# The order of the first two matmuls of a couple of units in the second product of a feed-forward phase

## Chip, cores and metric

One core of one Trainium2 chip runs the whole program. The time is device microseconds of one execution; the figure for a kernel is the median over its runs, and one more execution, taken with the profiler, gives the trace.

## What is computed

For 2048 tokens of width 640, in float32: a layer norm without scale, local dilated attention with 32 heads of 20 (each token looks at 8 tokens, two apart, itself the first), and beside it a feed-forward network whose output, through a SiLU, gates the attention's output.

```python
xn = _layernorm(x, axis=-1)
s = _A_ref(xn, A_wqkv, A_wo)          # qkv, windowed softmax attention, output projection
g = _silu(_B_ref(xn, B_w1, B_w2))     # silu(xn @ w1) @ w2, hidden width 1536
return x + s * g
```

## The kernel before, in words

The tokens are cut into 4 groups of 512 (two halves of the sequence, odd and even tokens apart, since the attention steps by two), and each group into T = 4 tiles of 128 tokens. For each group the program runs a phase of the q, k and v products with the attention (`qkv_phase`), the output projection of the group before (`wo_phase`), and the feed-forward phase (`ffn_phase`); the last group's projection (`wo_last`) ends the program.

Every matrix product is made of three TensorE products, to keep float32 accuracy: each operand is split into a high and a low part, and high times high, low times high and high times low are summed in PSUM. A matmul's stationary operand is a 128 x 128 tile, loaded by a weight load of its own; the moving operand has 512, 384 or 256 columns.

The unit of weights is a block of 128 rows of a weight matrix with its two halves (`wh`, `wl`), in a ring of RING = 7 SBUF slots. Loads of later units go out as slots come free (`w_load`, line 397; from the second use on a DMA from GpSimd's queue, line 410).

`ffn_phase` (line 880) takes the 12 blocks of the hidden width two at a time; two blocks are a couple of units here. For a couple:

- `up(f)` (line 885), twice: 15 matmuls of 512 columns each (lines 893 to 895) make the block's 512 hidden values for all tokens in a `rot` bank of PSUM. ScalarE then writes SiLU of it to `sh` (line 899, the high part) and to `sf` (line 900); VectorE makes the low part `sl` (line 901).
- `down((f, f + 1))` (line 904): for both blocks and each of the 4 token tiles, `big` (line 911) multiplies the tile of `sh` with `wh` and with `wl`; then for both blocks `small` (line 922) multiplies `sl` with `wh`.

The output of a token tile has 640 columns, more than a PSUM bank holds, so each product with a weight half is a pair of matmuls, made by `tm_mm` (line 770): a wide piece of CA = 384 columns into a bank of the tile's own (line 774), and a narrow piece of CB = 256 columns into half of a bank that two tiles share (line 777). The argument `cols` says which of the two goes first:

```python
def tm_mm(banks, t, st, w, first, last, cols=(0, 1)):
...
    for k in cols:
        (wide, narrow)[k]()
```

A couple so has 24 pairs (16 of `big`, 8 of `small`), 48 matmuls behind 30 matmuls of 512 columns. Before the change every pair of `down` takes the wide piece first, but for the last pair of a couple, which takes the narrow one first (`ends`, line 923).

The order of the work is set by a planner, `Weave` (line 63): each step is added with its engine, an assumed duration, the keys that it reads and writes, and a priority. TensorE's steps stay in the order in which they were added; the other engines' are chosen by a simulated clock. A `big` is one step for the planner, whatever the order inside it. The steps behind an entry into `down` are in these groups: `first` (line 890) of the couple's second block, then `big` with t = 0 of the first block.

Of the kernel before, what the change touches and what calls it, by code (L numbers as in the profile page):

```python
# [54 lines left out]
def tsl(t):  # L55
    return slice(t * P, (t + 1) * P)
# [157 lines left out]
def local_attention_silu_ffn(ctx: ExitStack, tc: tile.TileContext, x, wqkv, wo, w1, w2, out):  # L214
# [84 lines left out]
    def act(n, fn, reads, writes, prio, table=None):  # L299
        add("ACT", ac(n), fn, reads, writes, prio, table=table)  # L300

    def pe(dur, fn, reads, writes):
        add("PE", dur, fn, reads, writes)
        clock[0] += dur
# [128 lines left out]
    def w_next(*want):  # L433

        i = used[0]
        assert units[i] == want and i < loaded[0], (units[i], want)
        used[0] += 1
        s, n = i % RING, width(want)
        return WR[s][:, :n], WR[s][:, n:2 * n], ("wh", s), ("wl", s)

    def w_done(n=1):
        for _ in range(n):
            w_load()
# [321 lines left out]
    def tm_banks(narrow_first=False):  # L765
        b = [bank() for t in range(T // 2)] if narrow_first else None
        a = [bank() for t in range(T)]
        return a, b or [bank() for t in range(T // 2)]

    def tm_mm(banks, t, st, w, first, last, cols=(0, 1)):  # L770
        a, b = banks
        h = t % 2
        def wide():
            nc.tensor.matmul(a[t][0][:, :CA], st, w[:, :CA], start=first, stop=last)  # L774

        def narrow():
            nc.tensor.matmul(b[t // 2][0][:, h * CB:(h + 1) * CB], st, w[:, CA:], start=first and h == 0,  # L777
                             stop=last, skip_group_check=True)
        for k in cols:
            (wide, narrow)[k]()  # L780
# [99 lines left out]
    def ffn_phase(g, i, ix, io):  # L880
        nxt = g + 1 if g + 1 < NG else None
        ps = tm_banks()
# [21 lines left out]
        def down(fs):  # L904
            ws = {f: w_next("w2", f) for f in fs}
            ko = [[a[t][1], b[t // 2][1]] for t in range(T)]
            for f in fs:
                sh, ksh = SH[f % 2], ("sh", f % 2)
                wh, wl, kh, kl = ws[f]
                for t in range(T):  # L910
                    def big(t=t, f=f, sh=sh, wh=wh, wl=wl):
                        tm_mm(ps, t, sh[:, tsl(t)], wh, f == 0, False)
                        tm_mm(ps, t, sh[:, tsl(t)], wl, False, False)
                    near = f == FC - 1 and t == 0
                    pe(2 * TM, big, [ksh, kh, kl], ko[t] + ["near"] * near)
                    if near:
                        act(1, lambda: nc.scalar.activation(SD[:, 0, 0:1], epst, AF.Silu), ["near"], [("sd", 0)], 0, "silu")
            for f in fs:
                sl, ksl = SL[f % 2], ("sl", f % 2)
                wh, wl, kh, kl = ws[f]  # L920
                for t in range(T):
                    def small(t=t, f=f, sl=sl, wh=wh):
                        ends = f == fs[-1] and t == T - 1
                        tm_mm(ps, t, sl[:, tsl(t)], wh, False, f == FC - 1, (1, 0) if ends else (0, 1))
                    pe(TM, small, [ksl, kh], ko[t])
                w_done()
# [64 lines left out]
```

## Time and profile before

| | |
|---|---|
| median of 3 runs | 620.53 us (619.21 to 621.4) |
| the profiled execution: its own time | 621.1 us |
| its span, from the first to the last instruction | 619.3 us |
| TensorE busy | 612.6 us, 3357 matmuls |
| VectorE busy | 562.9 us |
| ScalarE busy | 308.3 us |
| GpSimd busy | 113.4 us |
| mean DMA rate | 262 GB/s |

In the profile PE is TensorE's matmuls, PEld its weight loads, DVE VectorE, ACT ScalarE, POOL GpSimd and SP the queue that issues most DMAs. L774 is line 774 of the kernel; the helper `tm_mm` records both pieces of a pair there (L774 the wide one, L777 the narrow one), whoever calls it, so groups are told apart by the tile that they read: `sh` and `sl` are the second product of the feed-forward phase, `thl` the output projection or the q, k and v products. A row of the timeline has start, duration, engine, line and operation. A matmul's duration in it (279 to 390 ns) overlaps the next one's; the distance from one start to the next is what it takes of TensorE.

### The profile page before, as it was taken

To read this page: it belongs to the slowest core of one execution; us is meant where nothing else is said; L and a number is where in the kernel's file an instruction comes from. 1 tells how busy PE (TensorE), PEld (TensorE's weight loads), DVE (VectorE), ACT (ScalarE), POOL (GpSimd) and SP (SyncE) were. 2 spreads that over 40 slices of the span, in tenths; PEclk is the share of its full clock that TensorE was granted. 3 is DMA by queue.
4 is the path that set the end of the run, shared out by engine and by line. 5 is a ranking of instruction groups with operands and counts; after the bars stand their busy time and mean duration, and the time that the engine had idled before them with its cause. 6 is when DMAs were issued, how large, how long until landed. Compare 5 with 4: busy or idle time off the path is not lost.

```text
span 619.3 us, 9090 instructions
## 1 busy us (share of the span) xinstructions
PE 612.6 (99%) x3357; PEld 553.6 (89%) x3357; DVE 562.9 (91%) x581; ACT 308.3 (50%) x651; POOL 113.4 (18%) x168
## 2 busy tenths in 40 slices
PE   8999999999999999999999999999999999999997
PEld 7889899999889999999888999999988999999997
DVE  6449999999989999999998999999979999899974
ACT  5424657936476313861844602593396416153650
POOL 4510000001110133111222232311111213311100
PEclk9999999999999999999999999999999999999999
DMA  8989999876999997865699999865579999966642
GB/s 254 316 238 333 357 358 395 351 237 196 286 335 353 330 357 264 260 190 153 173 262 238 326 340 331 261 192 163 150 205 281 247 317 306 302 197 194 208 131 106
DMA packets 65449, 162.45 MB, mean 262 GB/s; under 512 B 7053, under 2 KB 29165, under 8 KB 65405
## 3 DMA queue, kind: packets, MB, share of 16 engines
q0 software_dynamic: 20016, 82.58, 44.6%
q1 hardware_dynamic: 45389, 79.29, 40.6%
q8 instruction: 26, 0.43, 0.3%
q14 instruction: 18, 0.15, 0.1%
HBM read 109.55 MB, written 34.16 MB: 232 GB/s over the span
## 4 chain that ended last, share of the span: by engine, by line
PE 88%; DMA 6%; SPq 3%; DVE 2%; issue 1%; ACT 0%; DVEq 0%
PE acc L774 22%; PE acc L777 14%; PE rot L895 8%; PE rot L894 8%; PE rot L893 8%; PE acc L747 8%; PE acc L746 8%; PE acc L745 8%; DMA half_q<-w 2%; DMA half_w<-w 1%; DMA kv<-kv 1%; SPq L384 1%; PE acc L684 1%; SPq L385 1%; DMA gate<-in_A_wqkv_dram 1%; PE rot L777 1%
## 5 line engine op out<-in xcount | busy, mean ns | idle before, releaser
L745 PE MATMUL acc<-w,thl 128*128 128x512 f32 (+1 forms) x300 | 112.5, 375 | 0.0
L747 PE MATMUL acc<-w,thl 128*128 128x512 f32 (+1 forms) x300 | 112.4, 375 | 0.0
L746 PE MATMUL acc<-w,thl 128*128 128x512 f32 (+1 forms) x300 | 112.4, 375 | 0.0
L774 PE MATMUL acc<-w,sh 128*128 128x384 f32 x384 | 111.6, 334 | 0.0
L777 PE MATMUL acc<-w,sh 128*128 128x256 f32 x384 | 107.1, 279 | 0.0
L899 ACT ACTIVATE sh<-rot 128x512 fp32r<-128x512 f32 x48 | 28.7, 597 | 150.2 <-PE rot L895 150.1
L895 PE MATMUL rot<-thl,w 128*128 128x512 f32 x240 | 93.6, 390 | 0.0
L894 PE MATMUL rot<-thl,w 128*128 128x512 f32 x240 | 93.6, 390 | 0.0
L893 PE MATMUL rot<-thl,w 128*128 128x512 f32 x240 | 93.5, 389 | 0.0
L617 DVE TENSOR_TENSOR pr<-e,kv 128x2560 f32<-128x2560 f32 x32 | 90.3, 2822 | 0.7
L579 DVE TENSOR_TENSOR pr<-q,kv 128x2560 f32<-128x2560 f32 x32 | 90.1, 2817 | 0.5 <-DMA kv<-kv 0.3
L582 DVE TENSOR_REDUCE l<-pr 128x128 f32<-128x2560 f32 x32 | 90.0, 2813 | 0.5
L622 DVE TENSOR_TENSOR pr<-pr 128x1280 f32<-128x1280 f32 x64 | 75.5, 1180 | 1.5
L774 PEld LDWEIGHTS acc<-w,sh 128*128 128x128 f32 x384 | 72.1, 188 | 1.1
L777 PEld LDWEIGHTS acc<-w,sh 128*128 128x128 f32 x384 | 72.2, 188 | 0.9
L410 POOL DMA_DIRECT2D w<-half_w x72 | 38.5, 534 | 188.0 <-PE rot L895 59.8
L410 POOL DMA_DIRECT2D w<-half_q x52 | 27.6, 531 | 239.9 <-PE rot L895 114.7
L745 PEld LDWEIGHTS acc<-w,thl 128*128 128x128 f32 x300 | 56.3, 188 | 8.9 <-ACT q L536 0.2
L746 PEld LDWEIGHTS acc<-w,thl 128*128 128x128 f32 x300 | 56.3, 188 | 8.7
L747 PEld LDWEIGHTS acc<-w,thl 128*128 128x128 f32 x300 | 56.3, 188 | 8.5
L774 PE MATMUL acc<-w,thl 128*128 128x384 f32 x225 | 63.1, 333 | 0.0
L495 ACT ACTIVATE xin<-sf 32x256 f32<-32x256 f32 (+1 forms) x144 | 54.6, 379 | 9.7 <-DVE sf L522 8.1
(92 smaller groups left out, 1042.7 us busy)
## 6 DMA issues: line engine op xcount, KB each, us to landing
w<-half_w POOLq DMA_DIRECT2D x72, 640.0 KB, 6.1
w<-half_q POOLq DMA_DIRECT2D x39, 512.0 KB, 4.7
half_w<-w SPq DMA_DIRECT2D x24, 640.0 KB
w<-half_wo POOLq DMA_DIRECT2D x15, 640.0 KB, 5.7
kv<-kv SPq DMA_DIRECT2D x15, 560.0 KB
half_q<-w SPq DMA_DIRECT2D x15, 512.0 KB
kv<-kv SPq DMA_DIRECT2D x15, 420.0 KB
gate<-in_B_w_dram SPq DMA_DIRECT2D x16, 320.0 KB
```

The costliest lines, as they stand in the source:

```text
L579: dve(2560, lambda t=t: nc.vector.tensor_tensor(out=PR, in0=win(qq[:, t:t + 2, :], W, 0), in1=win(kv[:, 0, t:t + 2, :], W, CQ), op=OP.mult ...
L582: dve(2560, lambda t=t: nc.vector.tensor_reduce(out=l[:, t:t + 2].rearrange("p t w h -> p (t w h)"), in_=PR.rearrange("p t w (h d) -> p (t ...
L617: dve(2560, lambda t=t, v=v: nc.vector.tensor_tensor(out=PR.rearrange("p t w (h d) -> p t (w h) d", d=DH), in0=e[:, t:t + 2].rearrange("p ...
L622: dve(2 * k * CQ, lambda k=k: nc.vector.tensor_tensor(out=PR[:, :, 0:k, :], in0=PR[:, :, 0:k, :], in1=PR[:, :, k:2 * k, :], op=OP.add), [] ...
L745: nc.tensor.matmul(o, hi, wh, start=c == 0, stop=False)
L746: nc.tensor.matmul(o, lo, wh, start=False, stop=False)
L747: nc.tensor.matmul(o, hi, wl, start=False, stop=c == DC - 1)
L774: nc.tensor.matmul(a[t][0][:, :CA], st, w[:, :CA], start=first, stop=last)
L777: nc.tensor.matmul(b[t // 2][0][:, h * CB:(h + 1) * CB], st, w[:, CA:], start=first and h == 0, stop=last, skip_group_check=True)
L893: nc.tensor.matmul(h, wh[:, cs], TH[i][:, c, :], start=c == 0, stop=False)
L894: nc.tensor.matmul(h, wh[:, cs], TL[i][:, c, :], start=False, stop=False)
L895: nc.tensor.matmul(h, wl[:, cs], TH[i][:, c, :], start=False, stop=c == DC - 1)
```

## The change

In `big`, the product of the high part with `wh` gets an order of its own. Where it is the very first pair of a couple (first block of the couple, first token tile) and the couple isn't the group's first one (`f` is not 0), the narrow piece goes ahead of the wide one. The pair behind it, with `wl`, keeps its order.

```diff
                     def big(t=t, f=f, sh=sh, wh=wh, wl=wl):
-                        tm_mm(ps, t, sh[:, tsl(t)], wh, f == 0, False)
+                        begins = f == fs[0] and t == 0 and f
+                        tm_mm(ps, t, sh[:, tsl(t)], wh, f == 0, False, (1, 0) if begins else (0, 1))
                         tm_mm(ps, t, sh[:, tsl(t)], wl, False, False)
```

Each group has 6 couples, of which 5 are changed: 20 in the program. VectorE's, ScalarE's, GpSimd's and SP's instructions stand as before.

TensorE, the second couple of group 0, before: the last two matmuls of `up`, then the couple's first pairs. `acc4` is the first token tile's own bank, `acc2` the one that it shares with the second tile, `w5` the ring slot of the couple's first unit, `sh0` the high part of its first block; in brackets the engines whose semaphores are waited for.

```order
L894 MATMUL rot1_112<-thl0_67,w4_78 128x512
L895 MATMUL rot1_112<-thl0_67,w4_78 128x512
L774 MATMUL acc4_109<-w5_79,sh0_82 128x384 [waits Activation_49]
L777 MATMUL acc2_107<-w5_79,sh0_82 128x256
L774 MATMUL acc4_109<-w5_79,sh0_82 128x384 [waits DVE_49]
L777 MATMUL acc2_107<-w5_79,sh0_82 128x256
L774 MATMUL acc5_110<-w5_79,sh0_82 128x384
```

TensorE at the same place, now:

```order
L894 MATMUL rot1_112<-thl0_67,w4_78 128x512
L895 MATMUL rot1_112<-thl0_67,w4_78 128x512
L777 MATMUL acc2_107<-w5_79,sh0_82 128x256 [waits Activation_49]
L774 MATMUL acc4_109<-w5_79,sh0_82 128x384
L774 MATMUL acc4_109<-w5_79,sh0_82 128x384 [waits DVE_49]
L777 MATMUL acc2_107<-w5_79,sh0_82 128x256
L774 MATMUL acc5_110<-w5_79,sh0_82 128x384
```

The first two of the couple have changed places, and the wait for ScalarE went to the one that is now first; the wait for VectorE (the low half of the weights) stays with the third. The wide bank is now written twice in a row.

TensorE, the second couple of group 1, before, where the weights come by a DMA (DMASW2 is its semaphore):

```order
L895 MATMUL rot_112<-thl_71,w_78 128x512
L774 MATMUL acc_107<-w_79,sh_82 128x384 [waits DMASW2_49,Activation_49]
L777 MATMUL acc_105<-w_79,sh_82 128x256
L774 MATMUL acc_107<-w_79,sh_82 128x384
L777 MATMUL acc_105<-w_79,sh_82 128x256
L774 MATMUL acc_108<-w_79,sh_82 128x384
```

TensorE at the same place, now:

```order
L895 MATMUL rot_112<-thl_71,w_78 128x512
L777 MATMUL acc_105<-w_79,sh_82 128x256 [waits DMASW2_49,Activation_49]
L774 MATMUL acc_107<-w_79,sh_82 128x384 x2
L777 MATMUL acc_105<-w_79,sh_82 128x256
L774 MATMUL acc_108<-w_79,sh_82 128x384
```

Both waits of the couple's first matmul went with its place, to the narrow piece. The 18 other changed entries have the same matmuls in the same orders; some lack the wait for VectorE or for the DMA.

## The prediction, made before the changed kernel ran

> **What bounds the kernel now.** I read the page first: the busy shares, the granted clock and the chain of work that ended last.
>
> ```profile
> span 619.3 us, 9090 instructions
> PE 612.6 (99%) x3357; PEld 553.6 (89%) x3357; DVE 562.9 (91%) x581; ACT 308.3 (50%) x651; POOL 113.4 (18%) x168
> PEclk9999999999999999999999999999999999999999
> PE 88%; DMA 6%; SPq 3%; DVE 2%; issue 1%; ACT 0%; DVEq 0%
> ```
>
> TensorE is busy in 99% of the span, at full granted clock in every slice, and 88% of the chain is TensorE work. VectorE's 91% looks close, but only 2% of the chain runs through it. The page warns that a busy PE is not a PE at its peak, because matmul ends are modelled; so every cost below is made from the start times of matmuls, not from their durations.
>
> Where does the rest of the chain lie? The chain in order of time shows its last DMA link, the last wait for VectorE, and the end:
>
> ```profile
> 64.79 9.13 DMA half_w<-w
> ...
> 74.05 0.69 DVE sl L901
> ...
> 611.36 2.60 PE acc L774 x15
> 613.95 1.72 PE acc L875 x15
> ```
>
> The last transfer in the chain ends at 64.79 + 9.13 = 73.92 us. From 74.8 to 615.7 us the chain is one unbroken row of matmuls. The first entry that the change touches is the second couple of group 0, in the timeline of TensorE:
>
> ```profile
> 83.81 0.39 PE L895 MATMUL rot<-thl,w 128*128 128x512 f32 x1
> 84.03 0.34 PE L774 MATMUL acc<-w,sh 128*128 128x384 f32 x1
> ```
>
> 84.03 us is behind that DMA. So each nanosecond that an entry gains or loses goes straight into the span: nothing hides it, and nothing else has to give way. The question is only how many nanoseconds the order of two matmuls is worth.
>
> The groups of instructions by line say whether TensorE ever waits at these lines:
>
> ```profile
> L774 PE MATMUL acc<-w,sh 128*128 128x384 f32 x384 | 111.6, 334 | 0.0
> L777 PE MATMUL acc<-w,sh 128*128 128x256 f32 x384 | 107.1, 279 | 0.0
> L774 PE MATMUL acc<-w,sl 128*128 128x384 f32 x192 | 57.4, 333 | 1.3 <-DVE sl L901 1.3
> ```
>
> The last column, idle time before the group, is 0.0 for all 768 matmuls that read `sh`, the first pair of every couple among them. The one wait of size (1.3 us) is in front of the `sl` matmuls, in the first couple of group 0, which the change leaves alone.
>
> **The change part by part.** In 5 of 6 couples of each of 4 groups, 20 in all, the first two matmuls change places. Nothing is added or removed: the same 48 matmuls, the same 48 weight loads, the same banks. TensorE's order goes from 512, 384, 256, 384, 256 to 512, 256, 384, 384, 256. No other engine's order moves, and no DMA.
>
> First, the wait that moves. It was on the 384-column piece and is now on the 256-column piece, which stands at the same place. What it waits for is ScalarE's `sh` of the couple's first unit, and past group 0 also the landing of that unit's weights. In the timeline of ScalarE:
>
> ```profile
> 217.89 0.60 ACT L899 ACTIVATE sh<-rot 128x512 fp32r<-128x512 f32 x1 [6.24 <-PE rot L895]
> ```
>
> That one ends at 218.49; the couple begins at 221.09 (below): 2.6 us to spare. For the landing there is no single row, but the 0.0 above covers it too. So the moved wait costs nothing before or after.
>
> Second, the spacing of the matmuls at an entry. This is the timeline of TensorE at the first couple of group 1 (its entry has the form of all 24); columns are start, duration, engine, line:
>
> ```profile
> 220.87 0.39 PE L895 MATMUL rot<-thl,w 128*128 128x512 f32 x1
> 221.09 0.34 PE L774 MATMUL acc<-w,sh 128*128 128x384 f32 x1
> 221.27 0.28 PE L777 MATMUL acc<-w,sh 128*128 128x256 f32 x1
> 221.39 0.34 PE L774 MATMUL acc<-w,sh 128*128 128x384 f32 x1
> 221.56 0.28 PE L777 MATMUL acc<-w,sh 128*128 128x256 f32 x1
> 221.68 0.34 PE L774 MATMUL acc<-w,sh 128*128 128x384 f32 x1
> ...
> 222.25 0.33 PE L774 MATMUL acc<-w,sh 128*128 128x384 f32 x1
> ```
>
> The fifth pair starts at 222.25, so the first four pairs took 222.25 - 221.09 = 1.16 us. To see what four pairs take undisturbed, I sum TensorE over stretches; the first is a stretch of 50 pairs in the output projection (the x in a column counts also the one or two matmuls that still run at its start), the second is a couple's 24 pairs, the third the 30 matmuls of 512 columns behind it, the fourth the next couple's 24 pairs:
>
> ```profile
> 199.76:214.09 14.33, 14.33 (x102) 14.33 (x101) 14.16 (x10) 7.48 (x16) 2.11 (x4) 1.00 1.10 337
> 221.09:227.99 6.90, 6.90 (x50) 6.89 (x49) 6.78 (x9) 1.09 (x2) 1.75 (x3) 1.00 1.07 406
> 227.99:234.81 6.82, 6.82 (x31) 5.63 (x31) 6.21 (x10) 1.09 (x2) 1.06 (x2) 1.00 0.95 303
> 234.81:241.71 6.90, 6.90 (x50) 6.89 (x49) 6.86 (x8) 3.95 (x5) 3.19 (x3) 1.00 0.71 250
> ```
>
> 14.33 / 50 = 0.2866 us for a pair; four make 1.146. The entry thus carries 1.160 - 1.146 = 0.014 us over the undisturbed stream. The whole down half of a couple carries 6.90 - 24 x 0.2866 = 0.02 us. That is all there is to win: at most 20 x 0.02 = 0.4 us, even if the new order made the half perfect. The 512-column half behind it begins 48 matmuls later, is preceded by the same matmuls as before, and doesn't change.
>
> What will the entry cost instead? Nowhere in this trace does a 256-column matmul follow a 512-column one, so I bound it by two rows. The nearest is the output projection, which enters with its narrow piece first, though out of a stream of 384:
>
> ```profile
> 197.06 0.28 PE L777 MATMUL acc<-w,thl 128*128 128x256 f32 x1
> ...
> 198.21 0.28 PE L777 MATMUL acc<-w,thl 128*128 128x256 f32 x1
> ```
>
> Four pairs take 198.21 - 197.06 = 1.15 us, 0.004 over the stream. If the new entry did as well, it would gain 0.010 us, times 20 = 0.2 us. The other end is an entry out of 512 columns into several 384-column matmuls on one bank, as the last quarter of the q, k and v products has it (here six of them), since the new order also puts two 384-column matmuls on one bank behind each other:
>
> ```profile
> 186.63 0.33 PE L745 MATMUL acc<-w,thl 128*128 128x384 f32 x1
> ...
> 187.70 0.33 PE L745 MATMUL acc<-w,thl 128*128 128x384 f32 x1
> ```
>
> Six steps take 1.07 us; undisturbed, by the chain's row above, six take 6 x 2.60 / 15 = 1.04. So this entry carries 0.03 us, 0.016 more than the present one; times 20 that is a loss of 0.3 us. Same-bank neighbours cost nothing by themselves: 2.60 / 15 = 0.1733 us there, against 0.17 to 0.18 for a 384-column step in the alternating rows.
>
> The sum runs from -0.4 to +0.3 us. I take -0.1: the narrow-first row is nearer in form (-0.2), but its step down in width is smaller than the one from 512, which speaks for less. Against the profiled execution's own time that is 621.1 - 0.1; the profiled execution lies 0.6 above the median of the runs shown, 620.53, and inside their spread, 619.21 to 621.4. So from the median: 620.5 - 0.1 = 620.4 us.
>
> Third, the weight load that stands behind a shorter matmul. The loads, from the page and from the timeline of PEld:
>
> ```profile
> L774 PEld LDWEIGHTS acc<-w,sh 128*128 128x128 f32 x384 | 72.1, 188 | 1.1
> 221.27 0.19 PEld L774 LDWEIGHTS acc<-w,sh 128*128 128x128 f32 x1
> 221.39 0.19 PEld L777 LDWEIGHTS acc<-w,sh 128*128 128x128 f32 x1
> ```
>
> Each load starts with the matmul in front of the one it serves. Now the couple's second load has the 384-column step, 221.27 - 221.09 = 0.18 us, to hide in; afterwards it has a 256-column step, 221.39 - 221.27 = 0.12. A load shows 0.188 us, more than either, yet the pairs keep to 0.2866 us, and the loads start 0.12 us apart and overlap one another in the records. So the 0.188 is latency, not occupancy, and a 256-column step hides a load already, in every pair. I cost this at nothing; if the cover failed, it is the second rival.
>
> The Trainium skill (TensorE: Matmul & The Clock Gate, section LDWEIGHTS) gives a load as the number of its columns divided by 1.2 GHz: an estimate of 107 ns for these 128 columns. By that the load fits under a 256-column step with some 10 ns left and the rival would cost nothing; a rule that speaks against putting a short matmul ahead of a load stops just short of biting here. By the recorded 188 ns the rival would cost 1.5 us.
>
> **The rivals.** One: no measurable change, which is the forecast; it takes in everything from -0.4 to +0.3 us, that is 620.1 to 620.8. What a measurement of this kernel can tell from no change is about 0.3%, 1.86 us, which is 1.86 / 20 = 0.093 us for each entry, six times what an entry carries now. Chance 0.93 (with it, that the change does less than it says: the first couples keep their order, so 20 of 24 entries move).
>
> Two, slower: the second load of the couple no longer hides. Behind a switch of tiles, from 512-column matmuls to a new `sh` and new weights, the load may not run as far ahead as in a steady stream. If its recorded 188 ns must fit under the 0.12 us step, 0.188 - 0.115 = 0.073 us come out for each entry, 20 x 0.073 = 1.5 us, 622.0, still under the bound. If it can't overlap at all, 20 x 0.188 = 3.8 us, 624.3. It decides from 0.093 us an entry on. For it: the one pair of widths that no row shows. Against it: in the entry of now the load at 221.27 sits under a 256-column matmul too, three matmuls behind the switch, and that step was 0.12 us like all others. Chance 0.03 for the full size.
>
> Three, faster by over 0.3%: it would need 0.093 us an entry, and the whole half holds 0.02. It can only come from elsewhere: the chain's DMA links, all before 74 us, differ from one execution to the next (the three runs span 2.2 us), without this change. Chance 0.03, and 0.01 more on the slow side for the same reason.
>
> **How the numbers follow.** Forecast 620.4 us. The range is set by the scatter of the runs more than by the change: from the lowest run, 619.2, to the highest with the upper bound of the cost added, 621.4 + 0.3 = 621.7. The second rival at full size lies outside with its 0.03. Faster by over 0.3%: 0.03; within: 0.93; slower: 0.04.
>
> **What would show it.** In the profile after, an entry should read 512, 256, 384, 384, with four pairs in 1.13 to 1.18 us, and a couple's 24 pairs in 6.88 to 6.92 us; idle before both `sh` groups stays 0.0, and the couple begins each 13.72 us (234.81 - 221.09) as now, to 0.02. The step behind the couple's first 256-column matmul tells of the second rival: about 0.12 us if the load hides, 0.19 and more if not. I am wrong if an entry moves by 0.093 us, or if idle time appears in front of a couple's first matmul.

## The result, and the profile after

The changed kernel takes 624.76 us (median of 4 runs, 624.61 to 625.38), the kernel before 620.2 us (median of 4, 619.21 to 621.4): a ratio of 1.0072, 95% interval 1.0052 to 1.0093. It is slower, by more than the 0.3% that a measurement of this kernel can tell. The forecast was 620.4 us and no change, at a chance of 0.93; the result lies outside the range.

The page of the changed kernel shows no new wait. TensorE has as many matmuls as before and is as busy (99%), at the same granted clock, in a span that is 3.8 us longer:

```profile
span 623.1 us, 9090 instructions
PE 617.5 (99%) x3357; PEld 558.8 (90%) x3357; DVE 561.7 (90%) x581; ACT 309.0 (50%) x651; POOL 112.9 (18%) x168
PEclk9999999999999999999999999999999999999999
PE 89%; DMA 6%; SPq 3%; DVE 1%; issue 1%; ACT 0%; ACTq 0%; DVEq 0%
```

The groups of the second product: idle time ahead of the `sh` matmuls is still 0.0, but the mean of one has grown, 334 to 340 ns for the wide piece, 279 to 281 for the narrow one. The third row stands for `sl`, whose matmuls the change doesn't touch; they went from 333 to 341.

```profile
L774 PE MATMUL acc<-w,sh 128*128 128x384 f32 x384 | 112.3, 340 | 0.0
L777 PE MATMUL acc<-w,sh 128*128 128x256 f32 x384 | 108.0, 281 | 0.0
L774 PE MATMUL acc<-w,sl 128*128 128x384 f32 x192 | 59.2, 341 | 0.1
```

Now an entry, in the timeline of TensorE (the third couple of group 1; columns start, duration, engine, line; the row with x2 is the two wide pieces in a row):

```profile
248.53 0.39 PE L895 MATMUL rot<-thl,w 128*128 128x512 f32 x1
248.76 0.28 PE L777 MATMUL acc<-w,sh 128*128 128x256 f32 x1
248.88 0.51 PE L774 MATMUL acc<-w,sh 128*128 128x384 f32 x2
249.22 0.28 PE L777 MATMUL acc<-w,sh 128*128 128x256 f32 x1
...
249.93 0.34 PE L774 MATMUL acc<-w,sh 128*128 128x384 f32 x1
```

The entry itself is as forecast: four pairs in 249.93 - 248.76 = 1.17 us (1.16 before), and the step from the first narrow piece to the wide one is 0.12 us, as in every other pair, so the weight load that runs beside it adds nothing. The time went elsewhere. This is the end of the same couple, 40 matmuls later:

```profile
254.42 0.34 PE L774 MATMUL acc<-w,sl 128*128 128x384 f32 x1
254.60 0.28 PE L777 MATMUL acc<-w,sl 128*128 128x256 f32 x1
254.72 0.34 PE L774 MATMUL acc<-w,sl 128*128 128x384 f32 x1
254.90 0.28 PE L777 MATMUL acc<-w,sl 128*128 128x256 f32 x1
255.02 0.34 PE L774 MATMUL acc<-w,sl 128*128 128x384 f32 x1
```

From wide piece to wide piece it is 0.30 us, 0.18 and 0.12, where it was 0.2866 before. The sums over the fifth to the last pair of this couple, in the kernel before and in the changed one (from left: the stretch, its length, busy PE, busy PEld):

```profile
249.69:255.43 5.74, 5.74 (x43) 5.74 (x42) 5.51 (x4) 5.66 (x9) 0.53 (x1) 1.00 0.73 236
```

```profile
249.93:255.93 6.00, 6.00 (x43) 6.00 (x42) 5.75 (x5) 5.91 (x10) 0.53 (x1) 1.00 0.66 210
```

5.74 / 20 = 0.287 us a pair before, 6.00 / 20 = 0.300 now. So there are two steady rhythms of the same alternating matmuls, at the same clock and without idle time, 13 ns a pair apart; the changed couples run in the slower one to their end. A whole couple's 24 pairs take 7.17 us in place of 6.89. The sum over the 24 pairs of a changed couple of group 1:

```profile
234.76:241.93 7.17, 7.17 (x50) 7.17 (x48) 7.10 (x9) 3.95 (x5) 2.91 (x3) 1.00 0.67 219
```

All 20 changed couples start in the slow rhythm, and 19 keep it: 19 x 0.274 = 5.2 us. Against that stands the first couple of group 0, which the change doesn't touch and whose start and wait differ from trace to trace: that couple's half took 8.47 us in the profiled execution before and 7.29 in the one after, 1.2 us less, and the couple began 0.24 us earlier (at 68.74 and 68.50 us). 5.2 - 1.2 - 0.2 = 3.8 us, the difference of the spans. Put otherwise, from the end of that couple on the program takes 542.1 us before and 547.3 after.

The twentieth changed couple is the most telling. It is the fourth of group 1, where TensorE stalls for a moment in both kernels, at the start of the couple's second block. Here are the matmuls of the changed kernel, and below them ScalarE's `sh` of that block and the weight load of the block's first piece:

```profile
264.51 0.34 PE L774 MATMUL acc<-w,sh 128*128 128x384 f32 x1
264.70 0.28 PE L777 MATMUL acc<-w,sh 128*128 128x256 f32 x1
264.81 0.34 PE L774 MATMUL acc<-w,sh 128*128 128x384 f32 x1
265.00 0.28 PE L777 MATMUL acc<-w,sh 128*128 128x256 f32 x1
265.11 0.43 PE L774 MATMUL acc<-w,sh 128*128 128x384 f32 x1
265.38 0.28 PE L777 MATMUL acc<-w,sh 128*128 128x256 f32 x1
...
265.78 0.33 PE L774 MATMUL acc<-w,sh 128*128 128x384 f32 x1
265.95 0.28 PE L777 MATMUL acc<-w,sh 128*128 128x256 f32 x1
266.06 0.33 PE L774 MATMUL acc<-w,sh 128*128 128x384 f32 x1
```

```profile
264.44 0.60 ACT L899 ACTIVATE sh<-rot 128x512 fp32r<-128x512 f32 x1
...
265.09 0.19 PEld L774 LDWEIGHTS acc<-w,sh 128*128 128x128 f32 x1
```

Up to 265.11 wide pieces begin 0.30 us apart; that one takes 0.27 to the next matmul, a stall of 0.08; from 265.78 on they begin 0.28 to 0.29 apart. The load had waited for `sh`, which was ready at 264.44 + 0.60 = 265.04 us: it begins 0.09 us behind the matmul at 265.00, where elsewhere a load is recorded 2 to 4 ns behind the matmul ahead of it. Behind this stall the fast rhythm was back.

### The profile page after: what moved, and what is told of

The parts are those of the page before. It is cut to its first block, busy times and chain, and to the rows that moved or that the text cites. A ratio compares the mean times of both kernels' runs of the same rounds, so it can differ in the third digit from the quotient of the medians.

```text
span 623.1 us, 9090 instructions
## 1 busy us (share of the span) xinstructions
PE 617.5 (99%) x3357; PEld 558.8 (90%) x3357; DVE 561.7 (90%) x581; ACT 309.0 (50%) x651; POOL 112.9 (18%) x168
## 4 chain that ended last, share of the span: by engine, by line
PE 89%; DMA 6%; SPq 3%; DVE 1%; issue 1%; ACT 0%; ACTq 0%; DVEq 0%
PE acc L774 22%; PE acc L777 14%; PE rot L895 8%; PE rot L894 8%; PE rot L893 8%; PE acc L745 8%; PE acc L746 8%; PE acc L747 8%; DMA half_q<-w 3%; DMA half_w<-w 1%; DMA kv<-kv 1%; SPq L384 1%; SPq L385 1%; PE acc L684 1%; PE rot L777 1%
## 5 line engine op out<-in xcount | busy, mean ns | idle before, releaser
L622 DVE TENSOR_TENSOR pr<-pr 128x1280 f32<-128x1280 f32 x64 | 73.9, 1155 | 1.5
L777 PEld LDWEIGHTS acc<-w,sh 128*128 128x128 f32 x384 | 72.2, 188 | 0.9
L774 PEld LDWEIGHTS acc<-w,sh 128*128 128x128 f32 x384 | 70.6, 187 | 1.0
L774 PE MATMUL acc<-w,sl 128*128 128x384 f32 x192 | 59.2, 341 | 0.1
```

Of the source, the lines that this page charges most:

```text
L622: dve(2 * k * CQ, lambda k=k: nc.vector.tensor_tensor(out=PR[:, :, 0:k, :], in0=PR[:, :, 0:k, :], in1=PR[:, :, k:2 * k, :], op=OP.add), [] ...
```

## The experiments

Each was one execution with a profile, beside one of the kernel before (619.06 to 620.17 us). Their whole times are told, but the first couple of group 0 moves them by up to 3.3 us: it began at 67.96 to 69.63 us and its half took 6.89 to 8.50, so that it ended at 74.85 to 78.13 us over all traces. So the verdicts rest on the lengths of couples and projections, and several totals lie outside the range of the very theory that the lengths bear out. W, N and B stand for matmuls of 384, 256 and 512 columns. "Changed couples" are the 20 past a group's first; the other 4 keep the order of before in every kernel, and ran at 6.89 us where nothing stalled and nothing was moved in memory.

### What of the new order does it: the two wide ones in a row, or the narrow one first?

**All pairs narrow first** (B, N W, N W, ...). In `big` and `small`, for couples past the first:

```diff
-                        tm_mm(ps, t, sh[:, tsl(t)], wh, f == 0, False)
-                        tm_mm(ps, t, sh[:, tsl(t)], wl, False, False)
+                        cols = (1, 0) if fs[0] else (0, 1)
+                        tm_mm(ps, t, sh[:, tsl(t)], wh, f == 0, False, cols)
+                        tm_mm(ps, t, sh[:, tsl(t)], wl, False, False, cols)
...
-                        tm_mm(ps, t, sl[:, tsl(t)], wh, False, f == FC - 1, (1, 0) if ends else (0, 1))
+                        tm_mm(ps, t, sl[:, tsl(t)], wh, False, f == FC - 1, (1, 0) if ends or fs[0] else (0, 1))
```

> All 24 pairs of the 20 changed couples take the narrow piece first, so a 256-column matmul still stands behind the last 512-column one, but no two wide pieces stand in a row. Theory A (two wide matmuls in a row move the stream into a slower rhythm, 0.300 us a pair in place of 0.287, that holds to the couple's end): the rhythm stays at 0.287, a couple's 24 pairs take 6.87 to 6.92 us, the whole 619 to 621.5. Theory B (the narrow matmul behind the 512-column one does it): 0.300 us a pair, 7.15 to 7.20 us for 24 pairs, the whole 624 to 626.

Measured: 624.3 us; the last 16 pairs of the second couple of group 1:

```profile
236.26:241.06 4.80, 4.80 (x34) 4.80 (x33) 4.73 (x8) 1.79 (x3) 1.00 (x2) 1.00 0.52 191
```

4.80 / 16 = 0.300. There are no two wide pieces in a row in these couples, so theory A falls; B stands.

**A turned pair in the middle** (B, W N, W N, W N, W N, N W, W N, ...):

```diff
-                        tm_mm(ps, t, sh[:, tsl(t)], wh, f == 0, False)
+                        turned = f == fs[0] and t == 2 and f
+                        tm_mm(ps, t, sh[:, tsl(t)], wh, f == 0, False, (1, 0) if turned else (0, 1))
```

> The couple begins wide first as before; the one turned pair is the high-weight pair of the third token tile, so that the stream has two narrow and then two wide pieces in a row at the fifth pair. Theory A in its plain form (any two wide in a row): 0.287 us a pair up to there and 0.300 from there on, 20 pairs by 0.0133 = 0.25 us for a couple more, the whole 624 to 626. Theory A in its balance form (a wide double moves the rhythm one way, a narrow double back): no lasting change, 6.88 to 6.93 us for 24 pairs. Theory B: 0.287 all along, 619 to 621.5.

Measured: 621.14 us, 24 pairs in 6.89 us; the last 16:

```profile
237.16:241.75 4.59, 4.59 (x35) 4.59 (x33) 4.55 (x7) 1.86 (x3) 1.10 (x2) 1.00 0.53 197
```

4.59 / 16 = 0.287. A turned pair inside a running stream does nothing, which again speaks against the plain form of A.

**The second wide piece on another bank** (the second token tile's pair with `wh` goes ahead of the first tile's pair with `wl`):

```diff
+                        if f == fs[0] and f and t < 2:
+                            tm_mm(ps, t, sh[:, tsl(t)], wh, f == 0, False, (0, 1) if t else (1, 0))
+                            if t:
+                                tm_mm(ps, 0, sh[:, tsl(0)], wl, False, False)
+                                tm_mm(ps, 1, sh[:, tsl(1)], wl, False, False)
+                            return
```

> The couple begins narrow, wide, wide, narrow as the changed kernel does, but the second wide piece belongs to the second token tile, so that the two wide ones write different PSUM banks and read the same moving operand. Theory A and theory B both: 0.300 us a pair as in the changed kernel, about 7.17 us for 24 pairs, 624 to 626. Theory C (the double write to one bank does it): 0.287, 6.88 to 6.92 us, 619 to 621.5.

Measured: 624.44 us, 24 pairs in 7.16. It doesn't matter whether the two wide pieces write one bank; C falls.

**Turned back at once** (B, N W, W N, N W, N W, ...): as the changed kernel, and all pairs behind the second one narrow first.

```diff
+                        begins = f == fs[0] and t == 0
+                        tm_mm(ps, t, sh[:, tsl(t)], wh, f == 0, False, (1, 0) if fs[0] else (0, 1))
+                        tm_mm(ps, t, sh[:, tsl(t)], wl, False, False, (1, 0) if fs[0] and not begins else (0, 1))
...
-                        tm_mm(ps, t, sl[:, tsl(t)], wh, False, f == FC - 1, (1, 0) if ends else (0, 1))
+                        tm_mm(ps, t, sl[:, tsl(t)], wh, False, f == FC - 1, (1, 0) if ends or fs[0] else (0, 1))
```

> The couple begins narrow, wide, wide, narrow as the changed kernel does, and all later pairs are narrow first, so that two narrow pieces in a row follow at once and the wide double is taken back. Theory A, plain form: 0.300 us a pair to the couple's end, about 7.17 us for 24 pairs, 624 to 626. Balance form: back at 0.287 after the narrow double, 6.88 to 6.93 us, 619 to 621.5. Theory B: 0.300, about 7.17 us.

Measured: 626.47 us, 24 pairs in 7.17. So within a couple, two wide pieces and then two narrow ones leave the slow rhythm as it is, and two narrow and then two wide ones (the second experiment) the fast one. The balance form falls too.

### What stands ahead

**The last 512-column matmul cut into two of 256**, with the changed order (B, N N, N W, W N, ...):

```diff
-                    nc.tensor.matmul(h, wl[:, cs], TH[i][:, c, :], start=False, stop=c == DC - 1)
+                    if f % 2 and f > 1 and c == DC - 1:
+                        for k in range(2):
+                            nc.tensor.matmul(h[:, k * 256:(k + 1) * 256], wl[:, cs],
+                                             TH[i][:, c, k * 256:(k + 1) * 256], start=False, stop=k == 1)
+                    else:
+                        nc.tensor.matmul(h, wl[:, cs], TH[i][:, c, :], start=False, stop=c == DC - 1)
```

> The changed kernel, with the last 512-column matmul ahead of the 20 changed couples cut into two of 256, so that the couple's narrow first piece stands behind a 256-column matmul; the arithmetic is the same. Theory B (a narrow piece directly behind a 512-column matmul sets the slow rhythm): 0.287 us a pair, 6.87 to 6.92 us for 24 pairs, the whole 619 to 622. Theory B2 (it is the narrow-first start of the couple, with its new tiles and waits, whatever stands ahead of it): 0.300 us a pair, 7.15 to 7.20 us, 624 to 626.

Measured: 624.31 us, 24 pairs in 7.16. It was to separate B from B2 and didn't quite: the first half of the cut is itself a 256-column matmul behind a 512. The runs on the cut below settle it.

**One 512-column matmul more, in mid-couple**, its result thrown away: ahead of the second block of the changed kernel, which then begins wide first, and ahead of the second block of the kernel before, which then begins narrow first (`begins = f == fs[1] and t == 0 and fs[0]`). The added step:

```diff
+                if f == fs[1] and fs[0]:
+                    pe(0.0, lambda sh=sh, wh=wh: nc.tensor.matmul(
+                        ROT[0], sh[:, tsl(0)], wh[:, :TOK], start=True, stop=True), [ksh, kh], [("rot", 0)])
```

> The changed kernel with one more 512-column matmul ahead of the couple's second block in the 20 changed couples; its result is thrown away, and the block then begins wide first. Theory B: the first 8 pairs run at up to 0.300 us, the 512 sets the rhythm anew, and the pairs behind it run at 0.287; the 16 of them take 4.59 to 4.62 us. Theory B2 (a slow rhythm lasts until the couple ends): 0.300 to the end, the 16 pairs take 4.78 to 4.81 us. The added matmuls cost 20 x 0.23 = 4.5 us by themselves, so the whole is 625 to 627 by B and 629 to 631 by B2.

Measured: 629.12 us; the 16 pairs behind the added matmul take 4.80 us: the slow rhythm stays, in all of these couples but the one that stalls.

> The kernel before (couples begin wide first), with the same added 512-column matmul ahead of the second block, whose very first pair is then narrow first. Theory B: 0.287 us a pair up to the added matmul, 0.300 behind it; the 16 pairs behind it take 4.74 to 4.81 us, the whole 627 to 630. Theory B2 (only the entry into the couple matters): 0.287 to the end, 4.58 to 4.62 us, 624 to 626.

Measured: 626.88 us. The entry into the second block, and the 16 pairs behind it:

```profile
236.86 0.28 PE L777 MATMUL acc<-w,sh 128*128 128x256 f32 x1
236.98 0.39 PE L911 MATMUL rot<-w,sh 128*128 128x512 f32 x1
237.21 0.28 PE L777 MATMUL acc<-w,sh 128*128 128x256 f32 x1
237.32 0.51 PE L774 MATMUL acc<-w,sh 128*128 128x384 f32 x2
```

```profile
237.21:241.97 4.76, 4.76 (x33) 4.76 (x32) 4.69 (x8) 1.64 (x3) 0.86 (x2) 1.00 0.48 175
```

4.76 against 4.59: with a 512 and a narrow piece behind it the fast rhythm became the slow one, in mid-couple. The added matmul is the first that reads the second block's `sh` and weights, and it takes over the wait for them, so the narrow piece has neither a wait nor new tiles of its own. So it is no matter of the couple's beginning as such (B2 falls here). No run begins the second block narrow first without the 512, so what the 512 adds is not shown. And a 512 and a wide piece did not turn the slow one back (B missed there): the two directions are not alike.

One of the 20 went another way, again the fourth couple of group 1, where the stall now falls on the added matmul. Its entry, and the 16 pairs behind it:

```profile
265.27 0.50 PE L911 MATMUL rot<-w,sh 128*128 128x512 f32 x1
265.61 0.28 PE L777 MATMUL acc<-w,sh 128*128 128x256 f32 x1
265.73 0.51 PE L774 MATMUL acc<-w,sh 128*128 128x384 f32 x2
```

```profile
265.61:270.20 4.59, 4.59 (x34) 4.59 (x32) 4.29 (x5) 4.50 (x8) 0.53 (x1) 1.00 0.27 103
```

The 512 took 0.34 us in place of 0.23, and with the same order of pieces behind it the pairs stayed at 4.59 / 16 = 0.287. So a narrow piece behind a 512 does not always bring the slow rhythm.

**The output projection wide first**, everything else as before:

```diff
-                    tm_mm(banks, t, OH[i][:, c, tsl(t)], wh, c == 0, False, (1, 0))
-                    tm_mm(banks, t, OH[i][:, c, tsl(t)], wl, False, False, (1, 0))
+                    tm_mm(banks, t, OH[i][:, c, tsl(t)], wh, c == 0, False)
+                    tm_mm(banks, t, OH[i][:, c, tsl(t)], wl, False, False)
...
-                    tm_mm(banks, t, OL[i][:, c, tsl(t)], wh, False, c == DC - 1, (1, 0))
+                    tm_mm(banks, t, OL[i][:, c, tsl(t)], wh, False, c == DC - 1)
```

> The feed-forward phase is as in the kernel before; the output projection of groups 0 to 2, which follows a stream of 384-column matmuls and took its narrow pieces first, takes its wide ones first in all of its 75 pairs. Theory B, as it stands (a narrow piece behind 512 columns): nothing changes, 0.287 us a pair, 619 to 621.5. Theory B3 (the piece that differs more in width from what stands ahead sets the fast rhythm in one case and the slow one in the other: it is wide first that is slow behind 384 columns): 0.300 us a pair in 3 x 75 pairs, 3 us more, 622 to 624.5.

Measured: 621.65 us. A projection has 60 pairs (5 blocks of 12), not the 75 of the expectation. Its 60 pairs of group 0, before (narrow first) and here of group 1 (wide first):

```profile
197.06:214.27 17.21, 17.21 (x122) 17.21 (x122) 17.01 (x11) 10.13 (x24) 2.63 (x5) 1.00 1.10 344
```

```profile
347.01:365.00 17.99, 17.99 (x121) 17.99 (x121) 16.19 (x17) 2.45 (x6) 2.65 (x5) 1.00 1.15 355
```

17.21 / 60 = 0.287 and 17.99 / 60 = 0.300: the same two rhythms, but here, behind 384-column matmuls, it is wide first that is slow. The other two projections of each kernel took the same. B as it stood explains nothing of this; the outcome is that of B3. But wide first behind a 384-column matmul isn't slow everywhere: the last projection, whose order no kernel changes, begins so behind the last couple's final wide piece, and it ran at 0.287 us a pair in both of these kernels.

### Where the tiles lie

The kernel places `sh`, `sl` and the projection's stationary tiles 64 bytes past a multiple of 128 in each partition (the projection's by SHIFT = 16 columns, `sh` by what is allocated ahead of it); the weights start on multiples of 128. Does that matter? First 64 bytes of padding ahead of `sh`, under the changed order and under the order of before:

```diff
+    pad = sb.tile([P, 16], F32, name="pad")
     SH = tiles("sh", 2, [P, TOK], F32R)
```

> The changed kernel with 64 bytes of padding ahead of the sh and sl tiles, which start 64 bytes past a multiple of 128 in each partition and then start on one, as the weights in the ring do. Theory D (the two rhythms come from how the address of the stationary tile lies against that of the moving one, so the order of the pieces acts otherwise at another offset): the couples leave the 0.300 us a pair of the changed kernel; mirrored, they run at 0.287, 6.87 to 6.92 us for 24 pairs, the whole 619 to 621.5; at some third rhythm otherwise. Theory E (the rhythm is set by the order of widths and by what ran ahead; addresses don't matter): 0.300, 7.15 to 7.20 us, 624 to 626.

Measured: 625.05 us, 24 pairs in 7.20.

> The kernel before with the same 64 bytes of padding. Theory D, mirrored: wide first is now the slow order, 0.300 us a pair, 24 x 24 pairs by 0.0133 = 7 us more or somewhat less, 625 to 628. Theory E: 0.287 us a pair as before, 619 to 621.5.

Measured: 622.39 us, 24 pairs in 6.92. In the couples the offset changes 0.03 us and leaves the two rhythms as they were: D falls for them, E holds. One couple tells against leaving it at that. In the fourth of group 1, which stalls here too, the stall did not bring the fast rhythm back. Its last 16 pairs, with the changed order and the padding:

```profile
264.77:269.60 4.83, 4.83 (x34) 4.83 (x33) 4.53 (x5) 4.74 (x8) 0.53 (x1) 1.00 0.32 116
```

Without the stall, 0.04 us, that is 4.79, or 0.299 us a pair. A shorter stall, 0.02 us, did end the slow rhythm without the padding (the cut in 384 and 128 below). So the offset may have a part in what a stall does; no run tests it.

Then the projection's tiles without their shift, narrow first as before and wide first (by the edit of the projection above):

```diff
-    OH, OL = turned_tiles(0, SHIFT), turned_tiles(1, SHIFT)
+    OH, OL = turned_tiles(0, 0), turned_tiles(1, 0)
```

> The feed-forward phase as before; the stationary tiles of the output projection, which the kernel places 64 bytes past a multiple of 128, are placed on one, the narrow pieces still first. Theory D: the projection's pairs leave 0.287 us, 0.300 if mirrored: 3 x 75 x 0.0133 = 3 us more and the last projection's pairs, 622 to 624.5. Theory E: 0.287, 619 to 621.5.

Measured: 622.2 us.

> As the last one, and the projection of groups 0 to 2 takes its wide pieces first, which at the kernel's own offset ran at 0.300 us a pair. Theory D, mirrored: 0.287, 619 to 621.5. Theory E: 0.300 in 3 x 75 pairs, 622 to 624.5.

Measured: 620.58 us. The 60 pairs of group 1, in the one and the other:

```profile
347.86:365.46 17.60, 17.60 (x122) 17.60 (x121) 16.01 (x17) 2.45 (x6) 2.65 (x5) 1.00 1.17 360
```

```profile
346.25:363.84 17.59, 17.59 (x122) 17.59 (x121) 16.12 (x17) 2.45 (x6) 2.65 (x5) 1.00 1.14 358
```

17.6 / 60 = 0.293 in both: a third rhythm, and the order of the pieces no longer matters. So the address does take part, in the projection: D holds there in its loose form (another rhythm at another offset), not mirrored, and E falls. For the couples it is the reverse: with these 64 bytes and without, the couple that begins narrow first is the slow one.

### Who sets the couple's rhythm, and what resets it

The last 512-column matmul ahead of the changed couples cut again, now under both orders:

```diff
+                    if f % 2 and f > 1 and c == DC - 1:
+                        for p, e in ((0, 384), (384, 512)):
+                            nc.tensor.matmul(h[:, p:e], wl[:, cs], TH[i][:, c, p:e], start=False, stop=e == TOK)
...
```

> The changed kernel, with the last 512-column matmul ahead of the 20 changed couples cut into 384 and 128 columns; the arithmetic is the same. Theory F (the first change of width behind the stream of 512 sets the rhythm of all that follows; from 512 to 384 it is the fast one): 0.287 us a pair, 24 pairs in 6.86 to 6.93 us although the couple begins narrow first. Theory G (the couple's own first pair sets it, narrow first the slow one): 0.300, 7.14 to 7.20 us. The cuts themselves cost up to 20 x 0.06 = 1.2 us; so the whole is 619 to 622.5 by F and 624 to 627 by G.

Measured: 625.36 us, 24 pairs in 7.22; the last 16 in 4.80. Slow, as G says. (24 pairs lie 0.02 us above G's range; the cut's own cost is in them.) In the couple that stalls, the second block's first wide piece took 0.19 us to the next matmul in place of 0.18, and the fast rhythm was back behind it.

The same with ((0, 256), (256, 512)) and the order of before:

> The kernel before, couples wide first, with the last 512-column matmul ahead of the same 20 couples cut into two of 256. Theory F: the change from 512 to 256 sets the slow rhythm although the couple begins wide first, 0.300 us a pair, 24 pairs in 7.14 to 7.20 us, the whole 624 to 626. Theory G: 0.287, 6.86 to 6.93 us, 619 to 622.

Measured: 621.92 us, 24 pairs in 6.88. Fast, as G says; F falls with both. This also clears what the first cut left open: behind the same two 256-column matmuls a couple is fast if it begins wide (6.88) and slow if it begins narrow (7.16).

The cut in 384 and 128 with the order of before:

> The kernel before, wide first, with the last 512-column matmul cut into 384 and 128: the control of the cut. Both F and G: 0.287 us a pair, 6.86 to 6.93 us for 24 pairs, 619 to 622.5. If it is slow all the same, the cut's 128-column piece has an effect of its own, and the two runs with it say nothing between F and G.

Measured: 619.77 us, 24 pairs in 6.94, the last 16 in 4.59: the control is fast. The piece of 128 columns leaves a stall in both kernels with this cut (24 pairs are 0.05 us longer in each, 7.22 and 6.94 where 7.17 and 6.89 are taken without it); what comes first behind it decides.

Last, a stall made on purpose. The changed kernel, with a matmul of 128 columns, its result thrown away, ahead of the couple's second block, which begins wide first:

```diff
+                if f == fs[1] and fs[0]:
+                    pe(0.0, lambda sh=sh, wh=wh: nc.tensor.matmul(
+                        ROT[0][:, :P], sh[:, tsl(0)], wh[:, :P], start=True, stop=True), [ksh, kh], [("rot", 0)])
```

> The changed kernel with an added matmul of 128 columns, whose result is thrown away, ahead of the second block of the 20 changed couples; it is shorter than a weight load, so it should leave a short stall, and the block behind it begins wide first. Theory H (a stall sets the rhythm anew, by the piece that comes first behind it): the 16 pairs behind it take 4.58 to 4.63 us, 0.287 us a pair, the whole 620.5 to 624. Theory I (no stall that short does it, as the added 512 did nothing): 4.76 to 4.82 us, 625 to 628.

Measured: 624.56 us, 1.4 of them the wait in the first couple of group 0; the 16 pairs take 4.64 us, 0.01 above H's range. In the timeline:

```profile
237.51 0.34 PE L774 MATMUL acc<-w,sh 128*128 128x384 f32 x1
237.69 0.28 PE L777 MATMUL acc<-w,sh 128*128 128x256 f32 x1
237.81 0.34 PE L774 MATMUL acc<-w,sh 128*128 128x384 f32 x1
237.99 0.28 PE L777 MATMUL acc<-w,sh 128*128 128x256 f32 x1
238.11 0.23 PE L911 MATMUL rot<-w,sh 128*128 128x128 f32 x1
238.17 0.39 PE L774 MATMUL acc<-w,sh 128*128 128x384 f32 x1
238.40 0.28 PE L777 MATMUL acc<-w,sh 128*128 128x256 f32 x1
238.51 0.33 PE L774 MATMUL acc<-w,sh 128*128 128x384 f32 x1
238.68 0.28 PE L777 MATMUL acc<-w,sh 128*128 128x256 f32 x1
238.80 0.33 PE L774 MATMUL acc<-w,sh 128*128 128x384 f32 x1
```

0.30 us from wide piece to wide piece up to the added matmul; a step of 0.23 behind it, 0.05 us more than a wide piece takes; then 0.29 (238.51 to 238.80, and so on to the couple's end). Without the 0.05 us the 16 pairs took 4.59. So it came out as H says: here a stall of 50 ns and a wide start ended the slow rhythm. The added 512, which left no stall, did not do it.

The couple that stalls by itself bears this out in five traces with a wide first piece in the second block: it left the slow rhythm in the changed kernel, with the other bank, with both cuts under the changed order (7.03 to 7.04 us in each of these), and with the added 512 then wide. Where the second block begins narrow first in a slow couple (all pairs narrow first, turned back at once) the slow rhythm went on behind the same stall, and the couple took 7.22 us. Two traces speak against H as a rule: with the padding a stall and a wide piece left the couple slow, and with the added 512 then narrow a stall and a narrow piece left it fast.

Nor is a stall the only way out. In the kernel that turns back at once, the last couple of the program is slow to its end; behind it the last projection begins wide first, without a stall, on other tiles. Its first 15 pairs:

```profile
603.66:607.96 4.30, 4.30 (x31) 4.30 (x31) 1.29 (x2) 3.59 (x8) 0.00 (x0) 1.00 0.21 53
```

4.30 / 15 = 0.287, as in the kernel before.

## Why the prediction was wrong, point by point

- *That TensorE bounds the span and that each nanosecond of it counts*: right. The difference of the spans is made of nothing else, once the varying start and wait of the first couple are taken out.
- *The moved wait costs nothing*: right, by the steps at the entries. The 0.0 of idle time that I read it from is weaker than I took it to be: the stall in the fourth couple of group 1 is a wait for `sh` at these very lines, in both kernels, and the column shows 0.0 with it, since the load waits and the matmul behind it is recorded longer (0.43 us).
- *The entry's own cost*: right. Four pairs in 1.17 us, forecast 1.13 to 1.18.
- *The sum runs from -0.4 to +0.3 us*: this is the step that failed. I took the entry's cost as all that the change could cost, and both bounding rows were entries; behind the fourth pair I let the stream run on at 0.2866 us a pair, since all undisturbed pairs of the trace did. The runs show that the pair has a second steady rhythm of 0.300 us, which no row of before has, and that a couple's first piece chooses between them where no stall comes in. The missing term is 20 pairs x 0.013 us for each couple, 0.27 us, three times the 0.093 us from which I had reckoned a change to be measurable.
- *At most 0.4 us to win*: never tested by this result; it went the other way.
- *The second rival*, 624.3 us, came within 0.5 us of the measured median, by a mechanism that isn't there: it needed the step behind the first narrow piece to be 0.19 us or more, and it is 0.12. At its place, the entry, nothing was lost; its size was a coincidence.
- The range took its width from the scatter of the runs, which lies ahead of the second couple. It said nothing of a state that all 20 couples enter together.
- *The signs*: the two that were to show the prediction wrong (an entry that moves by 0.093 us, idle time in front of a couple) did not appear; both looked at the entry. What did show it are the lengths: 24 pairs in 7.17 us where 6.88 to 6.92 was forecast, and a couple each 248.76 - 234.76 = 14.00 us in place of 13.72.

What is shown: the first piece of a couple sets the rhythm (the two kernels, and the two cuts under both orders); a 512 and a narrow piece behind it in mid-couple turn the fast one into the slow one in 19 of 20 couples; the order of later pairs in the couple and the bank of the second wide piece change nothing, and 64 bytes of offset of `sh` don't change which start is the slow one; and a stall with a wide piece behind it ended the slow rhythm in six kernels, though not in the one with the padding. What stays open is why there are two rhythms, and what exactly carries a stream from one to the other, since a slow stream also turned fast at the last projection without a stall. The trace has the starts of matmuls and weight loads; in a steady stream a load is recorded 2 to 4 ns behind the matmul ahead of it in both rhythms, so it doesn't show which of the two waits for which. Open too is why the projection behind 384-column matmuls is fast narrow first, the reverse of the couples, and why its order stops to matter when its stationary tiles move by 64 bytes.

The Trainium skill (TensorE: Matmul & The Clock Gate, section Back-to-back issue gap) says that the spacing in a stream of loads and matmuls is set by both; its formula for the gap of a single, isolated matmul, columns divided by 2.4 GHz and 2.5 ns more, gives an estimate of 162.5 + 109.2 = 272 ns a pair in any order. The trace disagrees with that estimate: the same pair takes 287, 293 or 300 ns.

## What to carry to other kernels

A bound made at the place of an edit misses what the edit leaves behind it: where a long regular stream follows, look at its rhythm as well, many steps later, and price the whole stream. When a matmul stream alternates widths, its time for each pair need not be the sum of the two widths' own steps. Here the fast rhythm is that sum: 0.1733 us for a 384-column matmul among its like (2.60 / 15), about 0.1136 for a 256-column one (the 15 in a row at the end of the kernel before, L875, keep TensorE busy for 1.87 us, of which the last one's own 0.28 is taken off: 1.59 / 14), 0.287 together; the slow one is 13 ns over it. So find the pair's steady length in the trace, and treat a change of the order at the stream's start as able to change it. Where a stream is in a slow rhythm, compare the couples that stalled with those that didn't: here one of 20 gave the first hint in the very first trace, and the same couple in the later traces showed where that hint stops.

## What the runs showed of the hardware, unexpected

- Two or three steady rhythms for the same alternating matmuls of 384 and 256 columns at full granted clock without idle time: 0.287, 0.293 and 0.300 us a pair. Nothing in the page's shares tells of it (PE 99% in each); between the kernel before and the changed one it shows as 334 and 340 ns in the mean of a wide matmul.
- Ending a slow rhythm by adding work: a matmul of 128 columns in mid-couple took 0.06 us and left 0.05 us of stall, and the 16 pairs behind it then ran in 4.59 us in place of 4.80, so that the couple was 7.07 us long in place of 7.17.
- A stall can save more than it costs, or save nothing: with a stall of 0.08 us a couple of the changed kernel took 7.04 us in place of 7.17, and with one of 0.04 us and the padding 7.23 in place of 7.20.
- What varies from trace to trace lies ahead of the second couple: over the 18 traces the first couple of group 0 ended at 74.85 to 78.13 us and took 6.89 to 8.50, while all other unchanged couples took 6.89 to 6.92 but for the one that stalls.
